# Another order of the first loads, and the first block of a layernorm handled in two pieces, at the head of a convolution-plus-gated-linear kernel

## The chip, the cores and the metric

One core of a Trainium2 chip runs the kernel. The metric is device microseconds from one launch to its end, the median over several runs; a profiled execution of the same program gives the trace.

## The reference

Input x is 2048 rows of 640 values in bf16. Two branches work on its layernorm, and both are added to x:

```
xn  = (x - mean) / sqrt(var + 1e-5)                     # over the 640 columns
A   = xn * (fftconv(kv, ssm_k) + kv * ssm_D)            # kv = shift_conv(k, 4 taps) * v
B   = (sigmoid(xn @ w_gate) * (xn @ w_up)) @ w_down     # 640 -> 1728 -> 640
out = x + A + B
```

The long convolution of A runs over 2048 positions for each of the 640 columns.

## The kernel before, in words

The 2048 rows are 16 blocks of 128 rows; four blocks make a group t of 512 rows, and the 640 columns are five chunks c of 128. Branch B works group by group: for each of 13 full slices fc of 128 gate or up columns (and one shared last slice), five matmuls of 128 x 512 accumulate over the chunks (`product`, line 270), ScalarE takes the sigmoid of the gate product (`gate_ev`, 279), VectorE multiplies it with the up product into `hT` (`up_ev`, 285), and after the 14th slice `down_mm` (314) multiplies with w_down. Branch A's steps (tap products on VectorE, two transform stages on TensorE, and their way back) are woven between those of B by `ORDER`, a long string written out beforehand: each letter takes the next step of one chain, and the instructions go to their engines in just this order. Each engine works through its own queue in order.

The head, before that string, works on group 0 alone and is what the change touches. It runs as follows.

- **Loads** (lines 500 to 506). Transfers go out on the queues of SP and ScalarE. SP: the first half of block 0 of x, block 1, then columns 0 to 255 of w_gate, of w_up, columns 256 to 511 of w_gate, of w_up. ScalarE: the second half of block 0, then blocks 2 and 3. Eight semaphores count transfers in turn, so each transfer waits for the eighth one before it. Further weights, k, v and tables follow on SP's queue from `ORDER`.
- **Fillers** (`busy`, 513). TensorE multiplies a tile of zeros into a bank called idle, ten times 128 x 512, and twice more after the first block's transposes.
- **Layernorm** (lines 520 to 527). For each of the four blocks VectorE takes statistics of two halves (`ln_stats`, 210) and joins them (`ln_aggr`, 214), GpSimd takes the power -0.5 (`ln_pow`, 222), and VectorE normalises (`ln_xn`, 227). The statistics of block i stand ahead of the normalisation of block i - 1 in VectorE's queue.
- **Turning** (`turn`, `xn_mm` 241, `xn_ev` 245). TensorE transposes the five chunks of a normalised block into one PSUM bank pt; ScalarE copies it into `xnT` in two pieces, of three chunks and of two.
- **Quarters** (`quarters`, 261). The first two slices of gate (u = 0) and up (u = 1) are not computed with 512 columns but in four quarters of 128 columns, one for each block, as the blocks become ready: 80 matmuls of 128 x 128 between and after the transposes.

PSUM has two pools: `psC`, two buffers, for the idle bank, the transposes and later branch A's stages, and `psG`, four buffers, for the products of B. `sig` has two buffers.

The order at the head in TensorE's queue is: ten fillers, transposes of block 0, two fillers, then for block 0 to 3 the gate and up quarters, with the transposes of the next block put between. After it the long products begin with slice 2 of gate (fc = 2), then slice 2 of up.

## Time and profile before

| | us |
|---|---|
| median of 3 runs | 233.82 |
| the runs | 233.81, 235.02, 233.82 |
| profiled execution | 233.8 |
| its span, first to last instruction | 232.0 |
| TensorE busy | 227.7 (98%) |
| VectorE busy | 203.4 (88%) |
| ScalarE busy | 122.1 (53%) |

The span is what the trace covers; the rest of the profiled execution's own time lies around it. In the timeline each row has the start, the length from the first start to the last end of the merged instructions, engine and source line, the tile written and the tiles read, the count, and in brackets the idle time before with what ended it. A row of a matmul counts its tail as well, so the distance between starts is the better measure of its cost.

### The profile page before, as it was taken

To read this page: it belongs to the slowest core of one execution; us is meant where nothing else is said; L and a number is where in the kernel's file an instruction comes from. 1 tells how busy PE (TensorE), PEld (TensorE's weight loads), DVE (VectorE), ACT (ScalarE), POOL (GpSimd) and SP (SyncE) were. 2 spreads that over 40 slices of the span, in tenths; PEclk is the share of its full clock that TensorE was granted. 3 is DMA by queue.
4 is the path that set the end of the run, shared out by engine and by line. 5 is a ranking of instruction groups with operands and counts; after the bars stand their busy time and mean duration, and the time that the engine had idled before them with its cause. 6 is when DMAs were issued, how large, how long until landed. Compare 5 with 4: busy or idle time off the path is not lost.

```text
span 232.0 us, 5419 instructions
## 1 busy us (share of the span) xinstructions
PE 227.7 (98%) x2199; PEld 130.9 (56%) x2200; DVE 203.4 (88%) x359; ACT 122.1 (53%) x156; POOL 12.0 (5%) x24
## 2 busy tenths in 40 slices
PE   7999999999999999999999999999999999999995
PEld 2854446787454556667653444478653544446772
DVE  4546989989969999999999999998799999997773
ACT  2533222277365887665875847663555667752000
POOL 5210000021001100000011000000000000000000
DMA  6999999997999799989999999699989999374784
GB/s 194 319 292 288 220 256 353 228 171 180 325 230 305 222 369 201 287 183 211 266 331 268 228 368 283 183 222 180 282 235 287 290 257 253 113 162 123 226 264 136
DMA packets 93803, 56.79 MB, mean 245 GB/s; under 512 B 50964, under 2 KB 87890, under 8 KB 93650
## 3 DMA queue, kind: packets, MB, share of 16 engines
q1 hardware_dynamic: 93346, 56.03, 93.1%
q10 hardware_dynamic: 432, 0.41, 0.7%
q8 instruction: 17, 0.28, 0.5%
q14 instruction: 8, 0.07, 0.1%
HBM read 36.12 MB, written 18.35 MB: 235 GB/s over the span
## 4 chain that ended last, share of the span: by engine, by line
PE 96%; DMA 1%; DVE 1%; ACT 0%; SPq 0%; issue 0%
PE pd L314 27%; PE pu L270 24%; PE pg L270 24%; PE psb L487 4%; PE ps L375 4%; PE ps L373 4%; PE ps L417 3%; PE psa L446 3%; PE pg L291 2%; DMA x<-in_A_q_dram 1%; PE pg L261 1%; PE pu L261 1%; PE pt L241 1%; DVE st L210 0%; ACT xnT L245 0%; SPq L501 0%
## 5 line engine op out<-in xcount | busy, mean ns | idle before, releaser
L270 PEld LDWEIGHTS <-w 128*128 128x128 bf16 x500 | 46.6, 98 | 53.8 <-issue 4.3
L314 PE MATMUL pd<-wd,hT 128*128 128x320 bf16 (+2 forms) x447 | 66.1, 299 | 0.1
L270 PE MATMUL pu<-xnT,w 128*128 128x512 bf16 x250 | 62.2, 379 | 0.0
L270 PE MATMUL pg<-xnT,w 128*128 128x512 bf16 x250 | 62.2, 379 | 0.0
L314 PEld LDWEIGHTS <-hT 128*128 128x128 bf16 x448 | 41.7, 98 | 18.1 <-issue 2.4
L279 ACT ACTIVATE sig<-pg 128x512 bf16<-128x512 f32 x52 | 31.1, 601 | 29.2 <-PE pg L270 25.8
L285 DVE TENSOR_TENSOR hT<-sig,pu 128x512 bf16<-128x512 bf16 x52 | 34.9, 680 | 11.0 <-PE pu L270 5.7
L231 ACT CAST xz<-ps 128x1024 bf16<-128x1024 f32 x36 | 35.2, 1015 | 14.3 <-PE ps L417 14.1
L231 ACT CAST t<-ps 128x1024 bf16<-128x1024 f32 x24 | 23.9, 1013 | 20.1 <-PE ps L375 16.9
L432 DVE TENSOR_TENSOR xz<-xz 128x2048 bf16<-128x2048 bf16 x20 | 24.4, 1220 | 0.2
L375 PE MATMUL ps<-kvh,S1t 128*128 128x128 bf16 x160 | 21.7, 220 | 0.0
L373 PE MATMUL ps<-kvh,S1t 128*128 128x128 bf16 x160 | 21.6, 218 | 0.0
L351 DVE TENSOR_TENSOR tmp<-kx,sc 128x1024 bf16<-128x1024 bf16 x30 | 20.5, 683 | 0.3
L353 DVE TENSOR_TENSOR acc<-acc,tmp 128x1024 bf16<-128x1024 bf16 x30 | 20.4, 680 | 0.3
L319 DVE TENSOR_TENSOR x<-pd,x 128x320 bf16<-128x320 f32 (+2 forms) x32 | 15.1, 480 | 3.8 <-PE pd L314 3.6
L373 PEld LDWEIGHTS <-S1t 128*128 128x128 bf16 x160 | 15.5, 97 | 2.9 <-DVE kvh L356 0.4
L375 PEld LDWEIGHTS <-S1t 128*128 128x128 bf16 x160 | 15.4, 96 | 2.5
L210 DVE BATCH_NORM_STATS2 st<-x 128x6 f32<-128x320 bf16 x32 | 13.9, 477 | 2.2 <-DMA x<-in_A_q_dram 2.0
L231 ACT CAST TBt<-ps 128x1024 bf16<-128x1024 f32 x14 | 13.9, 1013 | 3.0 <-PE ps L375 3.0
L492 DVE TENSOR_TENSOR yx<-psb,xn 128x512 bf16<-128x512 f32 x20 | 13.7, 687 | 1.4 <-PE psb L487 0.8
L430 DVE STREAM_SHUFFLE xz<-xz 128x512 f32<-128x512 f32 x20 | 14.6, 728 | 0.0
L231 ACT CAST ao<-psa 128x1024 bf16<-128x1024 f32 x9 | 9.0, 1013 | 9.2 <-PE psa L446 6.9
(53 smaller groups left out, 157.8 us busy)
## 6 DMA issues: line engine op xcount, KB each, us to landing
t<-d SPq DMA_DIRECT2D x15, 512.0 KB, 6.3
d<-t SPq DMA_DIRECT2D x13, 512.0 KB, 5.7
d<-TBt SPq DMA_DIRECT2D x7, 512.0 KB, 6.5
d<-ao SPq DMA_DIRECT2D x6, 512.0 KB, 5.5
bi<-d SPq DMA_DIRECT2D x6, 512.0 KB, 4.8
kvh<-in_A_v_dram SPq DMA_DIRECT2D x10, 256.0 KB, 6.1
hn<-in_A_ssm_k_dram SPq DMA_DIRECT2D x20, 128.0 KB, 5.9
S1t<-d SPq DMA_DIRECT2D x4, 512.0 KB, 6.8
```

The source lines that it names most:

```text
L231: nc.scalar.copy(out=out, in_=in_)
L270: nc.tensor.matmul(pg[:, :], lhsT=w[:, c, u * UP + fc * P:u * UP + (fc + 1) * P], rhs=xnT[:, :, c, :], start=(c == 0), stop=(c == NC - 1))
L279: nc.scalar.activation(sig[fc][:, :], pgs[0, fc][:, :], ACT.Sigmoid)
L285: nc.vector.tensor_tensor(hT[:, fc, :], sig[fc][:, :], pgs[1, fc][:, :], ALU.mult)
L314: nc.tensor.matmul(pd[:, :], lhsT=hT[:, fc, bb * P:(bb + 1) * P], rhs=wd[:, fc, es], start=(fc == 0), stop=(fc == NFC - 1))
L319: nc.vector.tensor_tensor(x[:, 4 * t + bb, es], pds[bb, half][:, :], x[:, 4 * t + bb, es], ALU.add)
L351: nc.vector.tensor_tensor(d["tmp"][:, :, :], kx[:, lo + 3 - m:hi + 3 - m, :], sb(m), ALU.mult)
L353: nc.vector.tensor_tensor(d["acc"][:, :, :], d["acc"][:, :, :], d["tmp"][:, :, :], ALU.add)
L373: nc.tensor.matmul(ps[:, i, 0:P], lhsT=S1[:, h, b, :], rhs=cin[c]["kvh"][:, 0, b, :], start=True, stop=True)
L375: nc.tensor.matmul(ps[:, i, P:2 * P], lhsT=S1[:, h, b, :], rhs=hp[:, b // 2, b % 2, :], start=True, stop=True)
L430: nc.vector.stream_shuffle(z[:, 2, :, :].bitcast(F32), z[:, 1, :, :].bitcast(F32), swap)
L432: nc.vector.tensor_tensor(z[:, 1:3, :, :], z[:, 0:1, :, :].to_broadcast((P, 2, 8, P)), z[:, 1:3, :, :], ALU.mult)
```

## The change

Four things change, all in the head.

1. The loads: block 0 and block 1 of x go in halves on both queues; then SP's queue has w_gate 0 to 255, block 2, w_up 0 to 255, block 3, w_gate 256 to 511, w_up 256 to 511. ScalarE's queue has only the two halves.
2. Block 0 is normalised in two pieces (columns 0 to 383 and 384 to 639), and the pieces are transposed into two buffers of `psC` and copied from there one by one.
3. On VectorE the normalisation of block 2 stands ahead of the statistics of block 3, directly behind its own statistics.
4. The third slice of gate (fc = 2) is computed in quarters as well, into a bank of `psC`, and so drops out of the long products; in `ORDER` its two letters are taken out. Nine fillers instead of ten stand ahead, and none behind the first transposes. Transposes and quarters have a new order, written out.

```
-    def ln_xn(g, i):
+    def ln_xn(g, i, lo=0, hi=DM):
...
-        nc.vector.tensor_scalar(xn[:, b, :], x[:, b, :], d["mv"][:, i, 0:1], d["rstd"][:, i:i + 1],
+        nc.vector.tensor_scalar(xn[:, b, lo:hi], x[:, b, lo:hi], d["mv"][:, i, 0:1], d["rstd"][:, i:i + 1],
...
-    def quarters(u, i, lo, hi):
-        for fc in range(2):
+    def quarters(u, i, lo=0, hi=NC, fcs=(0, 1)):
+        for fc in fcs:
             if i == 0 and lo == 0:
-                pgs[u, fc] = psG.tile([P, 512], F32, name=("pg", "pu")[u], tag="g")
+                pgs[u, fc] = psC.tile([P, 512], F32, name="pg", tag="c") if fc == 2 else psG.tile([P, 512], F32, name=("pg", "pu")[u], tag="g")
...
-    for i in range(2):
-        (sync, nc.scalar)[i].dma_start(x[:, 0, 320 * i:320 * i + 320], xr[:, 0, 320 * i:320 * i + 320])
-    for b, eng in ((1, sync), (2, nc.scalar), (3, nc.scalar)):
-        eng.dma_start(x[:, b, :], xr[:, b, :])
-    for lo in (0, 256):
-        for u in range(2):
-            load_w(sync, lo, lo + 256, u)
+    for b in range(2):
+        for i in range(2):
+            (sync, nc.scalar)[i].dma_start(x[:, b, 320 * i:320 * i + 320], xr[:, b, 320 * i:320 * i + 320])
+    for u in range(2):
+        load_w(sync, 0, 256, u)
+        sync.dma_start(x[:, 2 + u, :], xr[:, 2 + u, :])
+    for u in range(2):
+        load_w(sync, 256, 512, u)
...
-    busy(10)
+    busy(9)
     for i in range(4):
         ln_stats(0, i)
-        if i:
-            ln_xn(0, i - 1)
+        if i == 1:
+            ln_xn(0, 0, 0, 3 * P)
+            ln_xn(0, 0, 3 * P, DM)
+        if i == 2:
+            ln_xn(0, 1)
         ln_aggr(0, i)
         ln_pow(0, i, i + 1)
-    ln_xn(0, 3)
-    turn(0)
-    busy(2)
-    for i in range(4):
-        m = 3 if i < 3 else NC
-        quarters(0, i, 0, m)
-        if i in (1, 2):
-            turn(i + 1)
-        if m < NC:
-            quarters(0, i, m, NC)
-        if i == 0:
-            turn(1)
-        quarters(1, i, 0, NC)
+        if i > 1:
+            ln_xn(0, i)
+    for lo, hi in ((0, 3), (3, NC)):
+        pt = psC.tile([P, NC, P], BF16, name="pt", tag="c")
+        for c in range(lo, hi):
+            nc.tensor.transpose(pt[:, c, :], xn[:, 0, c * P:(c + 1) * P], ident[:])
+        nc.scalar.copy(out=xnT[:, 0, lo:hi, :], in_=pt[:, lo:hi, :])
+    quarters(0, 0, 0, 3)
+    quarters(0, 0, 3)
+    turn(1)
+    quarters(1, 0)
+    quarters(0, 1, 0, 3)
+    turn(2)
+    quarters(0, 1, 3)
+    quarters(1, 1)
+    quarters(0, 2, 0, 3)
+    quarters(0, 2, 3)
+    quarters(1, 2)
+    turn(3)
+    for i in range(3):
+        quarters(0, i, fcs=(2,))
+    quarters(0, 3)
+    quarters(1, 3)
+    quarters(0, 3, fcs=(2,))
     for fc in range(2):
         gate_ev(0, fc)
         up_ev(0, fc)
+    gate_ev(0, 2)
...
     for t in range(4):
         for fc in range(0 if t else 2, 13):
-            step("g", gate_mm, t, fc)
-            step("s", gate_ev, t, fc)
+            if t or fc > 2:
+                step("g", gate_mm, t, fc)
+                step("s", gate_ev, t, fc)
             step("g", up_mm, t, fc)
             step("u", up_ev, t, fc)
```

More of the change, by code (lines that the diff above doesn't have):

```diff
@@ L660 @@
     ORDER = """
-    mmmZmmmmmmmmmTmmmmmmggsguggsggsuukkgggssukkggukksukkkgsgukkgggsgukkggsgsukkgukstgggukksuHHDmmmmkkggg
-    ukgukgaAlugaAwlPgaAlllueegaAlPgaAklleewHDkgaAugaAkKTwgaAukkKwgaAukkHgaAukkkggsgggnustgaukKKgghakAsul
-    rwAsakggluglsaksAugHggkAVrubkkkBlswKBukgggaTVsgpkusukawgDkHPlngAaAaskgAKwAkukgskpbgtkBsllBugauAkgagp
-    sAaguswVpakAguhkHHAgrgDkwcgVklguCkkraeCagAgkAbuBkuBkkggKgkbBKpggBaeualwukkggeIuurlTklAehrgwtVbBBggag
-    kAagpupswAagkuaKswrgpAAkaHAskWguHpDgakuVsAggswucglJukkgkrCsbgpBugaBaAgAWkkgsbspugPkrBgwpgsRnFkukgprc
-    wgCJusgbgusgpuBdBWppbqrgsdBlRuqgBcqlCggJbsggksuBupgllkBbBgrqkWBgeaaeAAuppwdgaduRegaIAgrugpaAqaeqggup
-    AwcCqpJguugdbgFBgbBqqgugBppdcpWCuJqgrpsgqbgBsuwFgrgqsbuBgpBRsuWgpdcpqqdguJgqCsrrbFBgsgRbugBBpdrsppug
-    cdCqugCqgbsgWBqpqggusrBRbpudgrgqWspBpBqcupdJsgCbgRBpgBqqguWgsppuqscCudgJsguqgqgRdWgoquuqoddRgggRqquq
-    guoqoggdoouqdgdqgqdqqqugoggqqugoooouooo
+    mmmZmmmmmmmmmTmmmmmmgguggsggsuukkgggssukkggukksukkkgsgukkgggsgukkggsgsukkgukstgggukksuHHDmmmmkkggguk
+    gukgaAlugaAwlPgaAlllueegaAlPgaAklleewHDkgaAugaAkKTwgaAukkKwgaAukkHgaAukkkggsgggnustgaukKKgghakAsulrw
+    AsakggluglsaksAugHggkAVrubkkkBlswKBukgggaTVsgpkusukawgDkHPlngAaAaskgAKwAkukgskpbgtkBsllBugauAkgagpsA
+    aguswVpakAguhkHHAgrgDkwcgVklguCkkraeCagAgkAbuBkuBkkggKgkbBKpggBaeualwukkggeIuurlTklAehrgwtVbBBggagkA
+    agpupswAagkuaKswrgpAAkaHAskWguHpDgakuVsAggswucglJukkgkrCsbgpBugaBaAgAWkkgsbspugPkrBgwpgsRnFkukgprcwg
+    CJusgbgusgpuBdBWppbqrgsdBlRuqgBcqlCggJbsggksuBupgllkBbBgrqkWBgeaaeAAuppwdgaduRegaIAgrugpaAqaeqggupAw
+    cCqpJguugdbgFBgbBqqgugBppdcpWCuJqgrpsgqbgBsuwFgrgqsbuBgpBRsuWgpdcpqqdguJgqCsrrbFBgsgRbugBBpdrsppugcd
+    CqugCqgbsgWBqpqggusrBRbpudgrgqWspBpBqcupdJsgCbgRBpgBqqguWgsppuqscCudgJsguqgqgRdWgoquuqoddRgggRqquqgu
+    oqoggdoouqdgdqgqdqqqugoggqqugoooouooo
     """
```

## The prediction

> **What bounds the kernel now.** I read the page first (busy time and chain), then who made TensorE wait over the whole span, then the timeline of the first 14 us, since the change touches nothing else.

> ```profile
> span 232.0 us, 5419 instructions
> PE 227.7 (98%) x2199; PEld 130.9 (56%) x2200; DVE 203.4 (88%) x359; ACT 122.1 (53%) x156; POOL 12.0 (5%) x24
> PE 96%; DMA 1%; DVE 1%; ACT 0%; SPq 0%; issue 0%
> PE idle L513 <- DVE st L123: 1.2, 1, 1.2
> PE pt L241 <- DVE xn L227: 0.2, 1, 0.2
> ```

> The last two rows are the whole list of TensorE's waits: 1.2 us before the first filler, 0.2 us before the first transpose. From then on TensorE never stands, so whatever moves the point at which the long products begin moves the end by the same amount, unless a later transfer runs out of slack. In the order of the built programs nothing differs behind the head, on any engine, except which semaphore counts a transfer and which of four equal buffers a product gets (still the one of four allocations before). So the whole forecast is a sum over the head, up to one common point: the start of the first 512-column **up** product, at 13.41 before.

> ```profile
> 1.18 4.45 PE L513 MATMUL idle<-hT 128*128 128x512 bf16 x10 [1.18 <-DVE st L123]
> 5.00 0.63 PE L513 MATMUL idle<-hT 128*128 128x512 bf16 x1
> 5.78 0.45 PE L241 MATMUL pt<-ident,xn 128*128 128x128 bf16 x5 [0.15 <-DVE xn L227]
> 6.27 0.76 ACT L245 COPY xnT<-pt 128x384 bf16<-128x384 bf16 x2 [3.62 <-PE pt L241]
> 6.55 0.10 PEld L261 LDWEIGHTS <-w 128*128 128x128 bf16 x1 [0.38 <-DMA w<-in_B_w_gate_dram]
> 6.80 0.72 PE L261 MATMUL pg<-xnT,w 128*128 128x128 bf16 x10
> 7.35 0.44 PE L241 MATMUL pt<-ident,xn 128*128 128x128 bf16 x5
> 7.69 0.73 PE L261 MATMUL pu<-xnT,w 128*128 128x128 bf16 x10
> 8.36 0.49 PE L261 MATMUL pg<-xnT,w 128*128 128x128 bf16 x6
> 6.80:12.30 5.50, 5.50 (x95) 5.36 (x95) 1.99 (x7) 3.10 (x9) 1.10 (x2) 1.00 1.12 326
> 12.33 1.24 PE L270 MATMUL pg<-xnT,w 128*128 128x512 bf16 x5
> 13.41 1.24 PE L270 MATMUL pu<-xnT,w 128*128 128x512 bf16 x5
> ```

> Ten fillers run until the last one issued at 5.00; block 0's transposes start at 5.78, their copy at 6.27, the first real product at 6.80. The stretch 6.80 to 12.30 holds 95 short matmuls in 5.50 us: 0.058 us each. Five long ones take 13.41 - 12.33 = 1.08 us.

> **Part 1: block 0 earlier.** The chain before the transposes is VectorE's and POOL's.

> ```profile
> 3.20 0.89 DVE L210 BATCH_NORM_STATS2 st<-x 128x6 f32<-128x320 bf16 x2 [2.04 <-DMA x<-in_A_q_dram]
> 4.12 0.22 DVE L214 BATCH_NORM_AGGREGATE mv<-st 128x2 f32<-128x15 f32 x1
> 4.49 0.89 DVE L210 BATCH_NORM_STATS2 st<-x 128x6 f32<-128x320 bf16 x2
> 4.50 0.56 POOL L222 TENSOR_TENSOR rstd<-mv,mhalf 128x1 f32<-128x1 f32 x1 [1.50 <-DVE mv L214]
> 5.29 0.43 DVE L227 TENSOR_SCALAR xn<-x,mv,rstd 128x640 bf16<-128x640 bf16 x1
> 5.64 0.22 DVE L214 BATCH_NORM_AGGREGATE mv<-st 128x2 f32<-128x15 f32 x1
> 5.77 0.82 DVE L210 BATCH_NORM_STATS2 st<-x 128x6 f32<-128x320 bf16 x2
> 6.53 0.45 DVE L227 TENSOR_SCALAR xn<-x,mv,rstd 128x640 bf16<-128x640 bf16 x1
> 1.19 3.28 DMA x<-in_A_q_dram
> ```

> The last row (from the chain) is block 1 on SP's queue: it lands at 4.47, so its statistics start at 4.49, although the aggregate issued at 4.12 would have let them go at 4.12 + 0.13 = 4.25 (0.13: from 5.64 to 5.77). Block 1 in halves on two queues, with nothing beside it, has 320 KB to move in all instead of the 480 KB that had moved by 4.47 (below), so it lands well ahead of 4.25. Statistics then issue for 0.76 (5.77 to 6.53), to 5.01, and block 0's normalisation is next held by POOL, whose power ends at 4.50 + 0.56 = 5.06: it starts at 5.09 instead of 5.29. Of 640 columns the first piece has 384; the whole one took 0.43 and lets the next instruction go after 0.35, so I put the piece at 0.30 (bounds: 0.6 of 0.43 = 0.26, and 0.43). With the 0.06 from its end (5.72) to the transposes (5.78), these start at 5.45. Three transposes instead of five save 2 x 0.058 of the 0.49 between transpose and copy (5.78 to 6.27): copy at 5.45 + 0.37 = 5.82. Copy to product stays 0.53 (6.27 to 6.80): first product at **6.35, gain 0.45**. The second piece follows within 0.25 on each engine, behind six matmuls worth 0.35, so it costs nothing. The filler taken away ends the fillers about 0.42 earlier and frees the second buffer in time; the two taken out behind the transposes only filled the wait for the copy.

> **Part 2: the third gate slice in quarters.**

> ```profile
> 13.61 0.60 ACT L279 ACTIVATE sig<-pg 128x512 bf16<-128x512 f32 x1 [0.84 <-DVE hT L285]
> 43.80 0.22 PE L373 MATMUL ps<-kvh,S1t 128*128 128x128 bf16 x1
> ```

> Twenty matmuls at 0.058 are 1.16, in place of 1.08: **+0.08**. Its bank in the other pool is let go by the third sigmoid, which ended at 14.2 before; that pool is first wanted again at 43.80, so this costs nothing. Without that cover it would cost one sigmoid, 0.6. Between the last quarters and the up product that needs the first gate bank there are now 15 short matmuls in place of 10, so that wait does not appear either.

> **Part 3: what block 2 behind the first weights costs.** This is the term that I cannot read off.

> ```profile
> 1.21 0.87 ACTq L503 DMA_DIRECT2D x<-in_A_q_dram  x2
> 2.15 0.53 SPq L190 DMA_DIRECT2D w<-in_B_w_up_dram  x1
> x<-in_A_q_dram ACTq DMA_DIRECT2D x1, 160.0 KB, 3.0
> w<-in_B_w_up_dram SPq DMA_DIRECT2D x1, 320.0 KB, 5.5
> 8.13 0.22 DVE L214 BATCH_NORM_AGGREGATE mv<-st 128x2 f32<-128x15 f32 x1
> 8.43 0.55 POOL L222 TENSOR_TENSOR rstd<-mv,mhalf 128x1 f32<-128x1 f32 x1 [0.69 <-DVE mv L214]
> 9.01 0.45 DVE L227 TENSOR_SCALAR xn<-x,mv,rstd 128x640 bf16<-128x640 bf16 x1 [0.66 <-POOL rstd L222]
> ```

> Before, block 2 went on ACT's queue at 1.21 and took 3.0 to land (4.2). Now it is SP's fourth transfer, issued about 2.15, where the first up weights stood, which took 5.5 (to 7.65). So it lands between 2.15 + 3.0 = 5.15 and 7.65. By bytes: when block 1 landed (4.47) both queues had moved about 240 KB each, 480; when the up weights landed (7.65), 1280 KB: 252 KB/us. Block 2 now ends at 800 KB: 4.47 + 320/252 = **5.74**, my value. By the same line the gate weights (640 KB) land at 5.1, the up weights (1120) at 7.0, block 3 at 7.65, the third gate slice (1600) at 8.9; wanted at 6.35, 7.3, 8.1 and 10.9.
> [...]

> Call the landing L. Block 2's statistics now stand on VectorE ahead of block 1's normalisation, which starts at L + 0.02 + 0.76; 0.49 later its transposes can start: L + 1.27 = 7.01. TensorE has done its first ten matmuls at 6.35 + 0.58 = 6.93, so it stands 0.08. From these transposes to the first quarter on them it was 8.36 - 7.35 = 1.01 before and stays so; six matmuls, 0.35, end at L + 2.63. Block 2's own normalisation now waits on VectorE for POOL, ahead of block 3's statistics: aggregate 0.36 behind block 1's, then 0.88 (8.13 to 9.01), that is L + 2.02, and transposes can start at L + 2.51, just ahead of TensorE. Block 3: statistics at L + 2.38, aggregate 0.92 later (3.20 to 4.12), normalisation 0.88 later, transposes from L + 4.67; TensorE comes to them at L + 2.63 + 39 x 0.058 = L + 4.89. So VectorE's new wait is covered, with 0.12 and 0.22 to spare. From block 2's transposes on, TensorE has 5+4+10+10+10+5+15+10+10+5 = 84 short ones, 4.87: the common point is at **L + 7.50 = 13.24, against 13.41: gain 0.17**.
> If L did not bind, the same sum from 6.93 gives 6.93 + 1.01 + 0.35 + 4.87 = 13.16, gain 0.25. At L = 7.65 it gives 15.15, a loss of 1.74.

> **Forecast.** The profiled execution took 233.8 us, 1.8 outside its span; the median is 233.82. 233.8 - 0.17 = **233.6**. About 0.5% (1.17 us) is what a measurement of this kernel can tell from no change; this gain is 0.1%.

> **Rival A: TensorE stays slow for longer (slower).** The same 512-column filler was issued 0.42 us apart until 5.00 (3.82 us for nine), and long products later 0.216 apart, at half the price, though the granted clock stands at 1.00 in both. The fast pace began between 5.00 and 5.78: the five transposes there take 0.45 with their tail. So it takes 3.8 to 4.6 us of work from 1.18. Now the fillers are one fewer and the two behind the transposes are gone: TensorE is empty from about 5.0 to 5.45 and again from about 5.8 to 6.35. If that breaks the count and it takes as long again from 5.45, the pace is slow until 9.3 to 10.0. Of that, about 3.3 us from 6.35 on is work at half speed, 1.65 lost; slower transposes add 0.2, and 0.2 goes back into waits that a slow TensorE does not feel: about 235.2 (234.8 to 235.6). It decides if a stand of 0.45 in some 4 us, about a tenth, is enough to break the count. One of the three runs, 235.02, lies 1.2 above the others, which is the size of such a delay; no profile shows why.
> [...]

> **Rival B: block 2 lands much later.** For it: 7.65 is a real row of the same queue slot, with 320 KB against 160. Against it: the bytes ahead. At L = 6.5 the time is 234.4; the loss passes 1.17 from L = 13.41 + 1.17 - 7.50 = 7.08 on (235.0), and at 7.65 it is 235.5.

> **Rival C: faster by over 0.5%.** The whole stretch from 5.45 to 13.16 has no stand left to remove, so it would take a comparison in which the kernel before is usually at its 235.02: then 233.6 is 0.6% less. That the change does not do what it says is excluded by the built order, where pieces, buffers and quarters stand as described.

> **Numbers.** Forecast 0.54 (233.3 to 234.0). Rival A 0.31, of which 0.26 over 0.5% and 0.05 within. Rival B 0.12, of which 0.04 over and 0.08 within. Rival C 0.03. Faster 0.03; same 0.54 + 0.05 + 0.08 = 0.67; slower 0.30. The range goes from 233.2 (the bound of 0.25 and as much again for the guessed piece and copies) to 235.5, which leaves out rival A's upper end and rival B's: under 2 in 10.

> **What would show it.** Right: first quarter product near 6.35, block 1's transposes near 7.0, all short matmuls 0.058 apart, the first long up product near 13.2, no new wait of TensorE later. Rival A: short matmuls some 0.11 apart past 6.35. Rival B: VectorE's third pair of statistics released by x after 6.5. The forecast is wrong if TensorE waits anywhere behind 14 us.

## The result, and the profile after

| | before | after |
|---|---|---|
| median, us | 233.81 | 235.28 |
| runs compared | 22 | 21 |
| ratio, 95% interval | | 1.0044 (1.0027 to 1.0061) |
| profiled execution, us | 233.8 | 235.36 |
| first long up product in that trace | 13.41 | 15.35 |

(Two runs were disturbed as a whole and are left out here and below: one of the changed kernel, 296 us, and one of the kernel before beside experiments 9 to 12, 824 us.) The changed kernel is slower where a gain of 0.1% was forecast.

The ratio is taken over the runs, not from the medians; the medians alone give 1.0063. The times of single runs of these kernels spread from 233.2 to 236.6 us, and much of what follows is about how many lie high, so I give that share beside each ratio. Of the changed kernel's 21 runs, 15 were over 234.6 us; of the 118 runs of the kernel before that stood beside it and the experiments, 19. Each run also has a mean granted clock of TensorE. In the trace of the changed kernel below, 3.41 us at half clock take 0.7% off it (the mean is 0.992), so I take a mean under 0.995 as a sign that the clock fell: 8 of the changed kernel's runs show it, all among the 15.

The page after. The row PEclk is the granted clock of TensorE in tenths, in slices of 5.8 us; the page before lacks it, because that trace holds no record of the clock:

```profile
span 233.6 us, 5445 instructions
PEclk9799999999999999999999999999999999999999
PE 95%; DMA 2%; DVE 1%; SPq 1%; issue 0%
```

The clock is short of full in the second slice only, 5.8 to 11.7 us. TensorE's waits over the whole span (line, what ended the wait, us in total, times, longest):

```profile
PE idle L514 <- DVE st L123: 1.2, 1, 1.2
PE pt L241 <- DVE xn L227: 0.9, 1, 0.9
PE pg L261 <- ACT xnT L537: 0.4, 1, 0.4
PE pt L536 <- DVE xn L227: 0.3, 1, 0.3
```

Before, the second to fourth rows were one row of 0.2. Where the 0.9 is, the timeline of the head shows. Its last row is from the chain that ended last and is block 2's transfer.

```profile
1.18 3.83 PE L514 MATMUL idle<-hT 128*128 128x512 bf16 x9 [1.18 <-DVE st L123]
5.35 0.54 PE L536 MATMUL pt<-ident,xn 128*128 128x128 bf16 x5 [0.33 <-DVE xn L227]
6.25 0.72 PE L261 MATMUL pg<-xnT,w 128*128 128x128 bf16 x10 [0.37 <-ACT xnT L537]
6.56 0.89 DVE L210 BATCH_NORM_STATS2 st<-x 128x6 f32<-128x320 bf16 x2 [0.88 <-DMA x<-in_A_q_dram]
7.36 0.43 DVE L227 TENSOR_SCALAR xn<-x,mv,rstd 128x640 bf16<-128x640 bf16 x1
7.85 0.51 PE L241 MATMUL pt<-ident,xn 128*128 128x128 bf16 x5 [0.88 <-DVE xn L227]
8.15 1.27 PE L261 MATMUL pu<-xnT,w 128*128 128x128 bf16 x10
10.82 1.06 PE L261 MATMUL pu<-xnT,w 128*128 128x128 bf16 x10
12.28 0.72 PE L261 MATMUL pu<-xnT,w 128*128 128x128 bf16 x10
15.35 0.38 PE L270 MATMUL pu<-xnT,w 128*128 128x512 bf16 x1
2.13 4.40 DMA x<-in_A_q_dram
```

The first product starts at 6.25. Block 2, issued at 2.13, lands at 6.53; its statistics stand ahead of block 1's normalisation, so block 1's transposes start at 7.85, and TensorE stands 0.88 for them. Then ten up matmuls take 1.27 where they take 0.72 with a full clock (12.28). The windows show the same; their last three columns are granted clock, share of the DMA engines and GB/s, and the first two after the bounds are their length and TensorE's busy time:

```profile
3.00:4.00 1.00, 1.00 (x4) 0.31 (x3) 0.95 (x3) 0.00 (x0) 0.00 (x0) 1.00 0.75 167
4.69:8.10 3.41, 1.83 (x22) 1.18 (x21) 2.34 (x8) 0.75 (x2) 0.84 (x3) 1.00 1.11 324
8.10:11.50 3.40, 3.40 (x36) 3.40 (x34) 1.91 (x5) 1.51 (x4) 1.00 (x2) 0.50 1.11 333
11.50:14.00 2.50, 2.50 (x47) 2.50 (x45) 0.00 (x0) 0.69 (x2) 0.00 (x0) 1.00 1.16 297
```

From 8.1 to 11.5 the clock is at half, and in the 3.41 us ahead of that TensorE had worked for 1.83. In this execution, then, the late landing and the lost clock come together. With L, the landing of block 2, at 6.53 the prediction's sum puts the first long up product at 6.53 + 7.50 = 14.03; it came at 15.35, and I put the 1.32 between down to the half clock.

### The profile page after: what moved, and what is told of

It is laid out like the page before. It is cut to its first block, busy times and chain, and to the rows that moved or that the text cites. A ratio compares the mean times of both kernels' runs of the same rounds, so it can differ in the third digit from the quotient of the medians.

```text
span 233.6 us, 5445 instructions
## 1 busy us (share of the span) xinstructions
PE 228.0 (98%) x2211; PEld 132.7 (57%) x2212; DVE 203.8 (87%) x360; ACT 122.0 (52%) x156; POOL 12.0 (5%) x24
## 4 chain that ended last, share of the span: by engine, by line
PE 95%; DMA 2%; DVE 1%; SPq 1%; issue 0%
PE pd L314 26%; PE pu L270 24%; PE pg L270 23%; PE psb L487 4%; PE ps L375 4%; PE ps L373 4%; PE ps L417 3%; PE psa L446 2%; DMA x<-in_A_q_dram 2%; PE pg L291 2%; PE pg L261 1%; PE pu L261 1%; PE pt L241 1%; DVE st L210 0%; SPq L502 0%; SPq L187 0%
## 5 line engine op out<-in xcount | busy, mean ns | idle before, releaser
L270 PEld LDWEIGHTS <-w 128*128 128x128 bf16 x495 | 46.1, 98 | 53.2 <-issue 4.3
L270 PE MATMUL pu<-xnT,w 128*128 128x512 bf16 x250 | 62.2, 379 | 0.0
L270 PE MATMUL pg<-xnT,w 128*128 128x512 bf16 x245 | 60.9, 379 | 0.0
L279 ACT ACTIVATE sig<-pg 128x512 bf16<-128x512 f32 x52 | 31.1, 601 | 29.2 <-PE pg L270 26.4
L285 DVE TENSOR_TENSOR hT<-sig,pu 128x512 bf16<-128x512 bf16 x52 | 34.9, 680 | 10.7 <-ACT sig L279 5.0
L373 PE MATMUL ps<-kvh,S1t 128*128 128x128 bf16 x160 | 21.6, 218 | 0.0
L373 PEld LDWEIGHTS <-S1t 128*128 128x128 bf16 x160 | 15.5, 97 | 2.6 <-DVE kvh L356 0.2
L210 DVE BATCH_NORM_STATS2 st<-x 128x6 f32<-128x320 bf16 x32 | 14.0, 478 | 2.7 <-DMA x<-in_A_q_dram 2.7
```

The source lines that it names most:

```text
L270: nc.tensor.matmul(pg[:, :], lhsT=w[:, c, u * UP + fc * P:u * UP + (fc + 1) * P], rhs=xnT[:, :, c, :], start=(c == 0), stop=(c == NC - 1))
L279: nc.scalar.activation(sig[fc][:, :], pgs[0, fc][:, :], ACT.Sigmoid)
L285: nc.vector.tensor_tensor(hT[:, fc, :], sig[fc][:, :], pgs[1, fc][:, :], ALU.mult)
L373: nc.tensor.matmul(ps[:, i, 0:P], lhsT=S1[:, h, b, :], rhs=cin[c]["kvh"][:, 0, b, :], start=True, stop=True)
```

## The experiments

At first I held the stand ahead of block 1's transposes for the cause (theory 1), and the missing fillers for the rival (theory 2, the prediction's rival A). Every ratio is against runs of the kernel before that were made beside the experiment. Their medians and their runs over 234.6 us: 233.79 and 8 of 35 beside experiments 1 to 4, 233.83 and 5 of 29 beside 5 to 7, 233.69 and 3 of 32 beside 9 to 12. The median of every changed version lies above these, by 0.2 us at the least, so a ratio near 1 says that the loss can't be told from nothing, not that there is none.

**1. Blocks 2 and 3 on ScalarE's queue**

```
-    for u in range(2):
-        load_w(sync, 0, 256, u)
-        sync.dma_start(x[:, 2 + u, :], xr[:, 2 + u, :])
-    for u in range(2):
-        load_w(sync, 256, 512, u)
+    for b in (2, 3):
+        nc.scalar.dma_start(x[:, b, :], xr[:, b, :])
+    for lo in (0, 256):
+        for u in range(2):
+            load_w(sync, lo, lo + 256, u)
```

> The changed kernel, with blocks 2 and 3 of x back on ScalarE's queue behind its half of block 1; fillers, pieces, VectorE's order and the third slice in quarters stay as changed. Theory 1 (block 2 lands at 6.53 because SP's queue alone carries it behind the first weights; TensorE then stands 0.9 us ahead of block 1's transposes, and the clock falls to half for one stretch): block 2 lands before 5.2, the stand is under 0.2, the granted clock stays at 1.00, and the time is 233.4 to 233.8, no slower than the kernel before. Theory 2 (the three fillers that are gone let the clock fall, whatever lands when): the stand goes, but the clock still falls in about half of the runs, and the time is 234.6 to 235.3.

Ratio 1.0008 (0.9978 to 1.0037), median 234.38, 5 of 12 over 234.6. In the trace the stand ahead of block 1's transposes is gone, as theory 1 said. Block 2 is in by 5.83, where its statistics start without a wait for it (expected before 5.2), and block 3 is late instead:

```profile
7.21 0.44 PE L241 MATMUL pt<-ident,xn 128*128 128x128 bf16 x5
8.83 0.89 DVE L210 BATCH_NORM_STATS2 st<-x 128x6 f32<-128x320 bf16 x2 [0.55 <-DMA x<-in_A_q_dram]
13.66 0.38 PE L270 MATMUL pu<-xnT,w 128*128 128x512 bf16 x1
```

The profiled execution, at the full pace from its first product at 6.66 on (ten in 0.72), took 233.68. But 5 of 12 runs lay high, one of them with the clock under 0.995, though the profile has no such stand. Theory 1 does not explain that, and the interval is wide enough for either.

**2. Fillers in the two gaps**

```
...
+    busy(1, pgs[1, 0])
     quarters(0, 0, 0, 3)
     quarters(0, 0, 3)
+    busy(4, pgs[1, 0])
     turn(1)
```

(Left out: `pgs[1, 0]`, the first up bank, is allocated ahead, and `busy` takes the bank that it writes into.)

> The changed kernel with one filler behind block 0's transposes and four ahead of block 1's transposes, written into an up bank before its first real product; loads as changed. Both theories say that the clock now stays full. Theory 1: block 2 still lands near 6.5 and block 1's transposes still start near 7.85, so by the sum of the prediction with L = 6.5 the first long up product starts near 14.0 and the time is about 234.4: better than the changed kernel, worse than before by 0.4 to 0.8. Theory 2: the whole loss is the clock's, so the time is 233.6 to 233.9.

Ratio 1.0001 (0.9976 to 1.0027), median 234.26, 2 of 12 over 234.6, no run with the clock under 0.995 (the changed kernel: 8 of 21). Block 1's transposes start at 7.63, still late, but the clock stays (ten products take 0.72 at 7.92). The first long up product comes at 13.68, ahead of theory 1's 14.0. That alone takes the ratio down to what the measurement can't tell from nothing, so I take the clock for most of the loss.

```profile
7.63 0.45 PE L241 MATMUL pt<-ident,xn 128*128 128x128 bf16 x5
13.68 1.24 PE L270 MATMUL pu<-xnT,w 128*128 128x512 bf16 x5
```

**3. The loads alone, in the kernel before**

```
-    for i in range(2):
-        (sync, nc.scalar)[i].dma_start(x[:, 0, 320 * i:320 * i + 320], xr[:, 0, 320 * i:320 * i + 320])
...
+    for b in range(2):
+        for i in range(2):
+            (sync, nc.scalar)[i].dma_start(x[:, b, 320 * i:320 * i + 320], xr[:, b, 320 * i:320 * i + 320])
...
```

> The kernel before with the changed order of loads alone (all twelve fillers, block 0 whole, two slices in quarters). Theory 1: block 2 lands near 6.5, block 1's transposes start near 7.85 instead of 7.35, block 2's normalisation waits for block 3's statistics as well; slower than before by 0.5 to 1.2 (234.3 to 235.0), more where the clock falls. Theory 2: with the fillers in place it is within 0.3 of before.

Ratio 1.0003 (0.9978 to 1.0029), median 234.54, 5 of 12 over 234.6; no run with the clock under 0.995. In its trace the landing is as in the changed kernel, 2.13 + 4.28 = 6.41, and the head is 0.57 later:

```profile
6.43 0.89 DVE L210 BATCH_NORM_STATS2 st<-x 128x6 f32<-128x320 bf16 x2 [0.74 <-DMA x<-in_A_q_dram]
7.72 0.45 PE L241 MATMUL pt<-ident,xn 128*128 128x128 bf16 x5 [0.27 <-DVE xn L227]
13.98 1.24 PE L270 MATMUL pu<-xnT,w 128*128 128x512 bf16 x5
```

The loads put the head back by about half a microsecond. With all twelve fillers in place the ratio can't tell their price from nothing (its interval reaches up to 0.68 us), though the median lies 0.75 above that of the kernel before. The profiled execution took 234.68, 0.88 more than before and so over 234.6, though its products run at the full pace from the first one at 6.73 (ten in 0.72): a run can lie high without the clock.

**4. VectorE's order undone**

```
-        if i == 2:
-            ln_xn(0, 1)
+        if i > 1:
+            ln_xn(0, i - 1)
         ln_aggr(0, i)
         ln_pow(0, i, i + 1)
-        if i > 1:
-            ln_xn(0, i)
+    ln_xn(0, 3)
```

> The changed kernel with VectorE's order as before: block 3's statistics ahead of block 2's normalisation. Under theory 1, block 3 lands at 8.1, so block 2's normalisation moves from 8.59 to about 8.95 and TensorE waits up to 0.3 more for it: within 0.4 of the changed kernel, 235.3 to 235.7, and the clock falls as often. If this edit were the costly one (a third theory), it would be back at 233.8.

Ratio 1.0030 (1.0003 to 1.0057), median 235.11, 10 of 12 over 234.6, 4 with the clock under 0.995: like the changed kernel. Undoing VectorE's order does not bring the time back, so it is not the cause.

**5. The loads undone, in the changed kernel**

> The changed kernel with the loads of the kernel before, and nothing else undone (nine fillers, pieces, VectorE's order, third slice in quarters). Theory 1 (the order of loads makes the stand, and the stand lets the clock fall): blocks 2 and 3 land by 5.6 again, no stand of TensorE over 0.3 after 6.8, no run with a granted clock under 0.995, and the time is within 0.3 of before. Theory 2 (the missing fillers alone): still slower by about 1, with the clock under 0.995 in a third of the runs.

The edit puts back the load lines of the kernel before. Ratio 1.0024 (1.0001 to 1.0047), median 234.43, 5 of 12 over 234.6, only one with the clock under 0.995. Theory 1 asked for within 0.3 us; the ratio says 0.56, with an interval from 0.02 us on, so this run alone does not refute it. Theory 2 had the clock under 0.995 in a third of the runs, and it was not. The profiled execution (235.21) shows the other way of being slow:

```profile
1.18 4.02 PE L513 MATMUL idle<-hT 128*128 128x512 bf16 x9 [1.18 <-DVE st L123]
7.00 1.23 PE L261 MATMUL pg<-xnT,w 128*128 128x128 bf16 x10 [0.35 <-ACT xnT L536]
8.55 1.27 PE L261 MATMUL pu<-xnT,w 128*128 128x128 bf16 x10
10.26 0.62 PE L241 MATMUL pt<-ident,xn 128*128 128x128 bf16 x5
10.93 0.72 PE L261 MATMUL pu<-xnT,w 128*128 128x128 bf16 x10
15.12 1.24 PE L270 MATMUL pu<-xnT,w 128*128 128x512 bf16 x5
```

TensorE does not stand ahead of block 1's transposes here. All nine fillers ran at half pace, and so did everything until 10.6, in the middle of block 2's transposes (0.107 from start to start before it, 0.056 behind it), although the clock column stands at 1.00 from 3.4 to 13.6. This is rival A of the prediction, the clock opening late: slow until 10.6 (forecast 9.3 to 10.0), 235.21 (forecast 235.2). That the time agrees to the hundredth is in part luck, for the head is 1.71 later than before and the end 1.41.

**6. Loads undone and twelve fillers**

The edit adds `busy(10)` for `busy(9)` and `busy(2, pgs[1, 0])` behind block 0's transposes; pieces, VectorE's order and the quarters are what is left of the change.

> As the last one, with ten fillers and two more behind block 0's transposes, so that only pieces, VectorE's order and the quarters of the third slice are left of the change. Head: first product near 6.6 (the gate weights land at 6.5), the first long up product at 13.2 to 13.4. The time is 233.5 to 233.8, the same as before, since a gain of up to 0.2 in the head is taken by the wait for a transfer of v near 127 to 130. If it is faster by more than 0.2, that wait is no bound.

Ratio 1.0001 (0.9978 to 1.0024), median 234.06 (expected 233.5 to 233.8), 2 of 12 over 234.6. With the three fillers back the 0.24% of the last experiment is not seen any more; the two intervals touch, so the pair alone does not prove it.

**7. The kernel before with nine fillers**

```
-    busy(10)
+    busy(9)
...
-    busy(2)
```

> The kernel before with nine fillers, and none behind the transposes: the change's fillers alone. Theory 1: the waits that they filled are 0.4 each and TensorE is busy for most of any stretch of 3.4 us, so the clock does not fall; within 0.3 of before. Theory 2 (rival A of the prediction): slower by 1 or more, 234.8 to 235.3, with short matmuls 0.11 apart past 6.35.

Ratio 1.0034 (1.0003 to 1.0065), median 234.92, 7 of 12 over 234.6, none with the clock under 0.995. Theory 1 asked for within 0.3 us here. The ratio says 0.8 us and the medians 1.09: the missing fillers alone cost about as much as the whole change. The interval reaches down to 0.07 us, so it is the ninth experiment, with three fillers fewer still, that puts theory 1 out of the question. The profiled execution of this one happened to be one of the good ones, 233.85, with the first long up product at 13.39, so in this execution, where the clock opened early, taking the fillers out cost nothing. Half pace ended there at 4.3: the nine fillers took 3.63, against 4.02 in the fifth experiment, where all ran at half pace. What the fillers change, then, is most likely how often it opens in time; no run shows that directly.

**8. The changed kernel once more**

> The changed kernel once more, for another profile. Both theories say that block 2 lands at 6.4 to 6.6 and that TensorE stands ahead of block 1's transposes until 7.7 to 7.9. Theory 1 says further that the time follows the clock: if the granted clock falls after the stand, about 235.4; if it does not, the first long up product starts at 14.0 and the time is near 234.2.

234.15 us. The stand is there (landing 2.13 + 4.61 = 6.74), the clock stays:

```profile
6.76 0.89 DVE L210 BATCH_NORM_STATS2 st<-x 128x6 f32<-128x320 bf16 x2 [0.99 <-DMA x<-in_A_q_dram]
8.05 0.45 PE L241 MATMUL pt<-ident,xn 128*128 128x128 bf16 x5 [0.85 <-DVE xn L227]
8.35 0.72 PE L261 MATMUL pu<-xnT,w 128*128 128x128 bf16 x10
14.10 1.24 PE L270 MATMUL pu<-xnT,w 128*128 128x512 bf16 x5
```

This separates the two costs. The prediction's sum with L = 6.74 gives 14.24; it was 14.10. In this pair of executions the stand is worth 0.69 in the head and 0.35 in the time; the clock, in the first profile, the other 1.2.

**9. The kernel before with six fillers** (`busy(6)`, none behind the transposes). From here on theory F is meant, a guess from the traces so far: the share of runs in which the clock opens in time follows from how much of a stretch of some 3.4 us TensorE works (in the changed kernel's trace the half clock lasted 3.41).

> The kernel before with six fillers and none behind the transposes. Theory F (what decides is how much of the stretch of about 3.4 us that happens to end between 5 and 8 us TensorE was busy; with fewer fillers more of the runs miss it and do one more stretch at half pace): slower than with nine fillers, by 1.2 to 2 against before (235.0 to 235.8 in the median), with most runs over 234.6. Theory 1 (only the stand ahead of block 1's transposes matters): as the kernel with nine fillers, 234.9, or as before.

Ratio 1.0062 (1.0035 to 1.0088), median 235.27, 10 of 10 over 234.6, as theory F said. In its trace (236.3 us) TensorE waits 1.7 for block 0, and ten products still take 1.25 at 7.30:

```profile
1.18 2.74 PE L513 MATMUL idle<-hT 128*128 128x512 bf16 x6 [1.18 <-DVE st L123]
5.65 0.71 PE L241 MATMUL pt<-ident,xn 128*128 128x128 bf16 x5 [1.73 <-DVE xn L227]
7.30 1.25 PE L261 MATMUL pg<-xnT,w 128*128 128x128 bf16 x10 [0.94 <-DMA w<-in_B_w_gate_dram]
```

**10. The changed kernel with twelve fillers** (as in the sixth experiment, loads as changed).

> The changed kernel with ten fillers and two behind block 0's transposes, nothing in the stand ahead of block 1's transposes. Theory F: the first opening of the clock is as in the kernel before, so runs that stay slow from the start (over 234.8 with the granted clock at 1.00) become rare; the stand of 0.9 stays, so the clock may still fall at its end in some runs (clock under 0.995), and the typical run is at 234.1 to 234.4, where the second profile of the changed kernel was. Theory 1: as the changed kernel, 235.3, with the clock under 0.995 in four runs of ten.

Ratio 1.0013 (0.9993 to 1.0032), median 234.08, 4 of 12 over 234.6, none with the clock under 0.995. The three fillers alone take the change from 1.0044 (1.0027 to 1.0061) to this, with its late landing left in. I had expected the clock to fall in some runs, and it did in none. But 4 of 12 high runs are not rare, as theory F had them. The profiled execution is one of the four (234.77), and the clock is not its reason: its products run at the full pace from the first one at 6.37 (ten in 0.72), and its mean granted clock is 1.00. Its head is 0.44 later than before, its end 0.97, and the rest is lost near 127, at a wait of TensorE that the kernel before does not have:

```profile
13.85 1.24 PE L270 MATMUL pu<-xnT,w 128*128 128x512 bf16 x5
127.79 0.66 PE L417 MATMUL ps<-xn,SMt 32*32 32x512 bf16 x16 [0.37 <-ACT ao L231]
```

**11. Halves of block 1, pieces, quarters and thirteen fillers** (the first experiment with `busy(10)`, `busy(2, pgs[1, 0])` behind block 0's transposes and `busy(1, pgs[1, 0])` ahead of `turn(1)`).

> Pieces, quarters of the third slice and block 1 in halves on both queues, with blocks 2 and 3 on ScalarE's queue, ten fillers, two behind block 0's transposes and one ahead of block 1's: the candidate for a version that is better than both. Theory F: few runs over 234.6, the typical run at 233.6 to 233.8, equal to before within 0.2%, because the gate weights land at 6.4 and the wait for v near 127 to 130 takes what the head gains. Over 0.2% faster would say that the head does pay.

Ratio 1.0009 (0.9989 to 1.0030), median 233.98 (expected 233.6 to 233.8), 1 of 12 over 234.6. None of these versions beats the kernel before.

**12. The kernel before with fourteen fillers** (`busy(4)` for `busy(2)`).

> The kernel before with four fillers behind block 0's transposes instead of two. Theory F: the two more end at about 6.95 where the clock is full, so the head starts 0.15 later in the typical run (233.7 to 233.9), and where it is not, they keep TensorE busy: fewer runs over 234.6 than the kernel before has; in the mean the same within 0.1%. Theory 1: only the 0.15 later start.

Ratio 1.0018 (0.9999 to 1.0037), median 234.21, 2 of 12 over 234.6. More fillers than twelve bring nothing that this can show, and theory F's fewer high runs do not show either (3 of 32 in the kernel before beside it).

All runs over 234.6 us by the number of fillers, whatever else differs:

| fillers | kernels | runs over 234.6 |
|---|---|---|
| 6 | ninth experiment | 10 of 10 |
| 9 | changed; experiments 1, 4, 5, 7, 8 | 42 of 70 |
| 12 | before | 19 of 118 |
| 12 to 14 | experiments 2, 3, 6, 10, 11, 12 | 16 of 72 |

High is not the same as half clock: of the six profiled executions over 234.6, four ran at half pace in the head (the changed kernel, experiments 4, 5 and 9), the two with twelve fillers (3 and 10) did not. The fall of an open clock (a mean under 0.995) comes above all where both parts of the change meet: 12 of 34 runs with nine fillers and the late block 2 (changed, experiments 4 and 8), 2 of 36 with nine fillers and no stand for a late block 2 (1, 5, 7), none of 36 with the late block 2 and twelve fillers or more (2, 3, 10). With six fillers and the old loads it is 2 of 10.

## Why the prediction was wrong, by its own steps

- **The fillers at nothing: the step that failed.** The text said that the two behind the transposes "only filled the wait for the copy" and that the tenth one going was free. In the sum they stood at nothing, and without them runs lie high: with nine in place of twelve some six in ten, with twelve about two. The experiments with 9 and 6 fillers in the old kernel show it without any other edit (1.0034 and 1.0062), and twelve fillers in the changed kernel bring its 1.0044 down to 1.0013. The price of rival A was right (235.2; the median is 235.28, inside the stated range because that took in rival A's price), its chance of 0.31 was too low for a median. Its path, a clock that opens late, is only part of it: 8 of the 15 high runs show a fall, and in the first profile the clock had opened and was lost again behind the stand, which the prediction did not have. For the other 7 no profile shows what they did. I took the profile of one execution in which the clock opened between 5.00 and 5.78 as what the kernel always does, though the run at 235.02 lay before me.
- **One execution and the next.** In the trace of the changed kernel the granted clock changes at 4.694 us (its first opening), 8.107, 11.521 and, behind TensorE's last work, 233.387: 1, 2 and 67 times 3.413 us behind the first. In the fourth experiment it falls at 7.97 and is back at 11.38, again 3.41. The first opening is not tied to the kernel: in the second profile of the changed kernel the nine fillers took 4.02 where they had taken 3.83, so the full pace came later there. The same kernel lost the clock in one execution and kept it in the other.
- **L: a term mis-sized.** Forecast 5.74, measured 6.53 and 6.74. 252 KB/us was taken from a trace in which the engines were full from 3 to 4 us (0.98, 303 GB/s), and that hole is new. In all eight profiles with block 1 in halves the stretch 3 to 4 us moved 122 to 185 GB/s, in all six with block 1 whole 301 to 328, wherever blocks 2 and 3 were queued:

```profile
3.00:4.00 1.00, 1.00 (x4) 0.30 (x3) 0.80 (x2) 0.00 (x0) 0.00 (x0) 1.00 0.98 303
3.00:4.00 1.00, 1.00 (x4) 0.32 (x3) 0.74 (x2) 0.00 (x0) 0.00 (x0) 1.00 0.80 156
```

The first row is the kernel before, the second the first experiment, with blocks 2 and 3 on ScalarE's queue. So this hole does not come from block 2's place on SP's queue. The landing did move: on ScalarE's queue block 2 was in by 5.83 (issued at 1.63), on SP's at 6.53 (issued at 2.13). How much of that is the queue and how much the later issue is not separated. Why so little moves there when block 1 comes in halves stays open; no run here tries it.
- **L as rival B** was priced at 234.4 for 6.5, and the second profile of the changed kernel took 234.15 with 6.74. The mechanism was right. By the sum, 6.74 gives 14.24 at the common point and 234.6 in the time; it is 0.14 too late at the first and 0.5 too long at the second.
- **"Moves the end by the same amount": wrong by up to 0.5, in both directions.** I had listed the waits of matmuls and not those of weight loads. Before, two of those near 127 and 129 wait for a transfer of v and for the product made of it; a kernel that comes 0.25 later (the first experiment) does not wait for them:

```profile
126.90 0.25 PEld L417 LDWEIGHTS <-SMt 32*32 32x32 bf16 x16 [0.42 <-DMA kvh<-in_A_v_dram]
129.66 0.10 PEld L373 LDWEIGHTS <-S1t 128*128 128x128 bf16 x1 [0.45 <-DVE kvh L356]
127.15 0.14 PEld L417 LDWEIGHTS <-SMt 32*32 32x32 bf16 x16 [0.42 <-issue]
129.50 0.10 PEld L373 LDWEIGHTS <-S1t 128*128 128x128 bf16 x1
```

The first two rows are the kernel before, the last two the first experiment. Head and end, against before: changed +1.94 and +1.56, its second profile +0.69 and +0.35, first experiment +0.25 and -0.12, second +0.27 and -0.10. Matched product by product, the first experiment is 0.25 behind the kernel before at 126, 0.14 at 128 and 0.01 at 131, so 0.24 of the 0.37 is given back at these two places. The third and the tenth experiment go the other way, +0.57 and +0.88, +0.44 and +0.97: they lose more at waits behind the head. The gain of 0.17 that was forecast would most likely have been spent on the wait for v; no profiled execution had a head that was earlier by more than 0.02, so that is only argued.
- **Right:** the first product (6.35 forecast; 6.25 and 6.49), VectorE's new wait covered, the third slice's bank for nothing, and in the changed kernel no new wait of TensorE's matmuls behind the head (the tenth experiment has one).

## What to carry to other kernels

Work that only fills a gap of TensorE can be worth its place: the kernel before took 1.0034 times its time with nine of its twelve fillers and 1.0062 with six. Before taking such work out, count TensorE's busy time in every stretch of 3.4 us around the gap (the half clock here lasted 3.41), wherever the stretch begins, and not only the gap. One profile shows one case of a kernel whose runs go from 233.56 to 236.04 us; look at the spread of the times, and at a second profile, before a term is called free. List the waits of weight loads too, and look for a transfer further on that sets its own time, before a gain at the head is carried to the end.

## What the runs showed of the hardware

- In the changed kernel's trace the clock fell though TensorE had stood no longer than 0.88 us at a time: of the 3.41 us ahead of the fall it had worked 1.83, with stands of 0.33, 0.37 and 0.88. The moments of the clock give the 3.41 us ahead of a change, or behind the first opening, and the windows TensorE's busy time in them, transposes counted (a bound at which nothing changed is stepped by 3.413, the distance in the changed kernel's trace, from a moment at which something did):

| run | stretch, us | TensorE busy, us | clock behind it |
|---|---|---|---|
| experiment 4 | 4.56 to 7.97 | 1.71 | falls |
| changed | 4.69 to 8.11 | 1.84 | falls |
| experiment 7 | 4.29 to 7.70 | 1.89 | stays |
| experiment 10 | 4.40 to 7.81 | 2.31 | stays |
| experiment 9 | 5.68 to 9.09 | 2.47 | does not open |
| experiment 1 | 2.88 to 6.29 | 3.02 | opens |
